# Whole-array gates for one chunk, a shorter first guess, and another choice of tiles in a fused attention and feed-forward kernel

## The chip, the core and the metric

The kernel runs on one core of a Trainium2 chip. The core has a matrix engine (TensorE, PE in the profile; its weight loads are listed as PEld), a vector engine (VectorE, DVE), a scalar engine for functions such as the exponential (ScalarE, ACT), a general engine (GpSimd, POOL) and a queue that issues transfers (SyncE, SP). The engines run at the same time and wait for each other through semaphores. Matmul results go to a memory of eight banks, each 128 partitions by 512 numbers of 32 bits. The metric is the device time of one execution in microseconds (us), the median of several runs.

## What is computed

One transformer block without learned norm weights: attention on normalised `x`, then a gated feed-forward layer on the normalised sum. `S` is 2048, `D` 640, with 32 heads of 20 and a feed-forward width of 1728; inputs and output are bfloat16.

```python
def _A_ref(x, wqkv, wo):
    ...
    scores = jnp.einsum("bhqd,bhkd->bhqk", q, k) * (Dh ** -0.5)
    p = _softmax(scores, axis=-1)
    o = jnp.einsum("bhqk,bhkd->bhqd", p, v)
    return (lambda x, *d: x.transpose(*d))(o, 0, 2, 1, 3).reshape(B, S, D) @ wo

def _B_ref(x, w_gate, w_up, w_down):
    g = jnp.einsum("bsd,df->bsf", x, w_gate)
    u = jnp.einsum("bsd,df->bsf", x, w_up)
    h = _gelu(g) * u
    return jnp.einsum("bsf,fd->bsd", h, w_down)

x = A_x
h = x + _A_ref(_layernorm(x, axis=-1), A_wqkv, A_wo)
h2 = h + _B_ref(_layernorm(h, axis=-1), B_w_gate, B_w_up, B_w_down)
```

## The kernel before

**Chunks, slots, tiles, units.** The 2048 query rows are cut into seven chunks of 512, 512, 256, 256, 256, 128 and 128 rows (`CHUNKS`, numbered 0 to 6). Heads are handled in eight groups of four. A slot is one chunk with as many groups as make 512 columns: eight slots each for chunks 0 and 1, four each for chunks 2 to 4, two each for chunks 5 and 6, 32 in all, numbered 0 to 31. A slot has 64 tiles of scores, each 128 keys by 512 columns, which fill one bank. Tiles are worked in units of two or three neighbouring banks. The string `PATS` (line 766) gives each slot one character: under `2` units of three and two tiles alternate, in banks 0 to 2 and 3 to 4; under `3` all units have three tiles, and the second bank set is 3 to 5.

**Who takes the exponential.** A unit's scores are one group of matmuls on quarter rows of the array (`unit`, line 851), then one ACT exponential over all its banks (line 862). In some units of three the third tile goes to DVE instead, which computes the exponential from integer and polynomial operations (`d_exp`, line 788): a pass out of the bank, then seven operations on a pair of tiles, or on a single one at the end of a slot. The string `DS` (line 767) gives each slot a hexadecimal digit: how many of its tiles go to DVE. They are spread over the slot's whole units of three, without the first and the last two (`d_units`, lines 924 to 932). The exponentials are multiplied with the values on quarter columns of the array (line 912) and summed in bank 6.

**Work in the background.** The projections of later groups and, after the last slot of a chunk, that chunk's output projection, norm and feed-forward layer (`post`, line 979) are mixed into the slots that follow, in the banks that attention leaves free (5 and 7; under `3` only 7). In `post`, `ln_rsqrt` (line 576) gives the inverse square root of the variance: for the input's norm and for the last chunk by ACT and a reciprocal, for chunks 0 to 5 by DVE operations on a few numbers, a first guess from the bits of the number and two rounds of Newton's method. `mms` (line 1036) makes the gate and up projections. Each of their matmuls is given in two forms: `quarters`, four matmuls of 32 output rows each (line 662), and `whole`, one matmul on the whole array (line 659). The planner takes the quarters (`mode="col"`) as long as score matmuls are left, and the whole form (`alt`) after them. The gates go from their bank to memory by a DVE copy (line 1081), and ACT's gelu follows for several banks at once.

**Chunk 5** is the one in `GT` (line 356). Its attention takes slots 28 and 29; its gates run during slots 30 and 31, and its gelu, up and down projections are held back (`later`, line 1124) until after the last exponential, at the head of the tail. The tail also holds all of chunk 6's `post`.

**What sets the order.** A planner at build time (`Sched.schedule`, line 98) walks through time with a fixed cost for each operation, takes the ready operation of the highest priority on each engine (scores and exponentials first, then sums with the values, then epilogues, then background), gives out banks and so fixes the order of each engine's instructions. A change of the array's mode between `row`, `col` and `full` is charged 0.1 us (`MODE_SWITCH`, line 31). On the chip each engine works through its list in that order and waits where something is not ready. [...]

Of the kernel before, what the change touches and what calls it, by code (L numbers as in the profile page):

```python
# [6 lines left out]
ALU = mybir.AluOpType  # L7
# [3 lines left out]
I32 = mybir.dt.int32  # L11
# [39 lines left out]
class Sched:  # L51
# [10 lines left out]
    def op(self, eng, fns, dur, prio, reads=(), writes=(), acq=(), rel=(), after=(), sem=None, lat=None, mode=None, mb=0.0, alt=None):  # L62
        if self.evp is not None and eng == "dve" and rel and prio >= P_EPI:
            prio = self.evp
        o = Op()
        o.i = len(self.ops)
        o.eng, o.dur, o.lat, o.sem = eng, dur, LAT[eng] if lat is None else lat, sem
        o.mode = mode
        o.mb = mb
        o.alt = alt  # L70
        o.tag = writes[0] if writes else None
        o.fns = fns if isinstance(fns, list) else [fns]
        o.prio = (prio, o.i)
        deps = set(after)
        for r in reads:
            if r in self.lw:
                deps.add(self.lw[r])
        for w in writes:
            if w in self.lw:
                deps.add(self.lw[w])  # L80
            deps.update(self.rd.get(w, ()))
        for r in reads:
            self.rd.setdefault(r, []).append(o.i)
        for w in writes:
            self.lw[w] = o.i
            self.rd[w] = []
        deps.discard(o.i)
        o.deps = deps
        o.acq = list(acq)
        o.rel = list(rel)  # L90
        o.succ = []
        o.ready = 0.0
        o.start = None
        o.group = None
        self.ops.append(o)
        return o.i
# [230 lines left out]
RSQRT_MAGIC = float(0x5F3759DF)  # L327
# [25 lines left out]
XLAG = 0.85  # L353
XLG0 = 0.5
HG = 1
GT = (5,)
XPL = 1
KPR = 3.0
# [6 lines left out]
def bass_sequential_preLN__mha_block__glu_gated_geglu__prompt_kernel(  # L365
# [12 lines left out]
    with ExitStack() as es:  # L378
        sc = Sched(nc)
        op = sc.op  # L380
# [4 lines left out]
        def I(method, *args, **kwargs):  # L385
            return lambda eng: getattr(eng, method)(*args, **kwargs)  # L386


        def c_mm(n, passes=1):
            return 0.003 + passes * n / 2400.0  # L390
# [92 lines left out]
        def bank(b, n=512):  # L483
            return PS[:, 512 * b.b:512 * b.b + n]
# [91 lines left out]
        def ln_rsqrt(t0, n, prio, need_nm=0):  # L576
            ts = range(t0, t0 + n)
            y, v = rs[:, t0:t0 + n], mv[:, t0:t0 + n, 1]
            a, b = nw[:, 0, 0:n], nw[:, 1, 0:n]
            vk, rk = [("mv", t) for t in ts], [("rs", t) for t in ts]  # L580
            d = lambda fn, r, w: op("dve", fn, 0.14, prio, reads=r, writes=w)
            if need_nm:

                op("act", I("activation", a, v, ACT.Sqrt, bias=epsc[:, 0:1]), 0.19, prio, mode="sqrt", reads=vk + ["eps"], writes=["nw0", "sd"])
                d(I("reciprocal", y, a), ["nw0"], rk)
                if need_nm == 1:
                    d(I("scalar_tensor_tensor", out=nm[:, t0:t0 + n], in0=y, scalar=-1.0, in1=mv[:, t0:t0 + n, 0],
                        op0=ALU.mult, op1=ALU.mult), rk + vk, [("nm", t) for t in ts])
                return
            d(I("tensor_scalar", a, v, LN_EPS, None, ALU.add), vk, ["nw0"])  # L590
            d(I("tensor_scalar", b.bitcast(I32), a.bitcast(I32), 1, None, ALU.logical_shift_right), ["nw0"], ["nw1"])
            d(I("tensor_scalar", y.bitcast(I32), b.bitcast(I32), -1.0, RSQRT_MAGIC, ALU.mult, ALU.add), ["nw1"], rk)
            for _ in range(2):
                d(I("tensor_tensor", b, y, y, ALU.mult), rk, ["nw1"])
                d(I("scalar_tensor_tensor", out=b, in0=b, scalar=-0.5, in1=a, op0=ALU.mult, op1=ALU.mult),
                  ["nw0", "nw1"], ["nw1"])
                d(I("scalar_tensor_tensor", out=y, in0=b, scalar=1.5, in1=y, op0=ALU.add, op1=ALU.mult),
                  ["nw1"] + rk, rk)

        def ln_apply(eng, src, dst, dkey, t, rkeys, prio):  # L600
# [32 lines left out]
        def sc_id():  # L633
            _id[0] += 1
            return _id[0]
# [4 lines left out]
        for t0 in range(0, NT, 4):  # L640
            sa = [t for t in range(t0, t0 + 4) if LNS[t] == "act"]
            for t in range(t0, t0 + 4):
                (ln_stats_act if t in sa else ln_stats)(x_sb[:, t, :], t, [xkey(t)], P_EPI)
            if sa:
                assert sa == list(range(sa[0], sa[-1] + 1))
                op("dve", I("tensor_scalar", mv[:, sa[0]:sa[-1] + 1, 1], mv[:, sa[0]:sa[-1] + 1, 1], 1.0 / D, None, ALU.mult), 0.14,
                   P_QK, reads=[("mv1", t) for t in sa], writes=[("mv", t) for t in sa])
            ln_rsqrt(t0, 4, P_QK, 1)
            for t in range(t0, t0 + 4):
                e_ops.append(ln_apply(LNE[t], x_sb[:, t, :], xn_p[:, t % 4, :], ("xnp", t % 4), t, [xkey(t)], P_QK))  # L650
                transposes(xn_p[:, t % 4, :], [("xnp", t % 4)], xnT[:, :, t * 128:(t + 1) * 128], ("xnT", t),
                           ALLB, P_EPI, LNV[t])
                e_ops.append(len(sc.ops) - 2)
# [5 lines left out]
        def whole(out, l, r, start, stop):  # L659
            return [lambda eng: eng.matmul(out()[0:l.shape[-1]], l, r, start=start, stop=stop, skip_group_check=True)]  # L660

        def quarters(out, l, r, start, stop):
            m = l.shape[-1]
            return [lambda eng, j=j: eng.matmul(out()[j:j + 32], l[:, j:j + 32], r, start=start, stop=stop,  # L664
                                                tile_position=(0, j), skip_group_check=True) for j in range(0, m, 32)]
# [97 lines left out]
            tiles += [(s_, g, kb, j) for g in gs for kb in range(NT // nk) for j in range(4)]  # L763
            slot_end.append(len(tiles))

        PATS = '22222222222322232222222332223322'
        DS = '06418768558877797888786986867867'
        PAT = [((0, 1, 2), (3, 4, 5)) if PATS[i] == '3' else ((0, 1, 2), (3, 4)) for i in range(len(slots))]
        units, ubank, upos = [], [], []
        i = 0  # L770
# [154 lines left out]
        for s_, (c, gs) in enumerate(slots):  # L925
            us = [u for u, tl in enumerate(units) if len(tl) == 3 and all(x[0] == s_ for x in tl)]
            n = int(DS[s_], 16)
            us = us[1:len(us) - DTAIL]
# [50 lines left out]
        def post(c, banks, tail):  # L979
            p = P_EPI if tail else P_BG - PRE * (c >= PREC)  # L980
            q0, nq = CHUNKS[c]
# [10 lines left out]
            for tt in range(nt):  # L992
# [10 lines left out]
                for hf in range(2):  # L1003
                    bk = Bank(*banks)
# [11 lines left out]
            if tail:  # L1016
                op("act", I("activation", nm[:, 0:1], off0[:], ACT.Gelu_apprx_tanh), 0.06, -1, mode="gelu", reads=["off0"],
                   writes=["pre"], after=(sc.lw["sd"],))
# [5 lines left out]
            p, pre = P_BG - TFIRST * tail, p  # L1024
# [11 lines left out]
            def mms(k, w, wkey, after, p=p):  # L1036
                bk, key = Bank(*banks), ("bk", sc_id())
                for fi in range(min(fn_, NF - k * fn_)):
                    f = k * fn_ + fi
                    mf = min(128, DFF - 128 * f)  # L1040
                    for a in range(NA):
                        st = fi == 0 and a == 0
                        op("pe", quarters(lambda fi=fi: bank(bk)[:, fi * nq:(fi + 1) * nq], w[:, a, f * 128:f * 128 + mf],
                                          hnT[:, a, hb * 128:hb * 128 + nq], a == 0, a == NA - 1),
                           c_mm(nq), p, mode="col", alt=whole(lambda fi=fi: bank(bk)[:, fi * nq:(fi + 1) * nq],
                                                              w[:, a, f * 128:f * 128 + mf], hnT[:, a, hb * 128:hb * 128 + nq],
                                                              a == 0, a == NA - 1), reads=hk + [wkey], writes=[key], acq=[bk] if st else [],
                           after=after if st else ())
                return bk, key

            def wid(k):
                return min(512, NF * nq - 512 * k)
# [16 lines left out]
            else:  # L1069

                cp, gl = [], []
                for k in range(nb):
# [3 lines left out]
                    w_ = wid(k)  # L1076
                    if k >= nb - HG and c not in GT:
                        hold.append((k, bg, kg, m, fv, fk, w_))
# [3 lines left out]
                                 reads=[kg], writes=fk, rel=[bg], after=first))  # L1082
# [39 lines left out]

            if c in GT:
                def later(ba):
                    banks[:] = ba
                    gate_after[:] = [last_exp[0]]
                    rest()
                    down(GDP)
# [8 lines left out]
        if XPL:  # L1137
            op("act", I("activation", nm[:, 0:1], off0[:], ACT.Exp, scale=0.0), 0.06, P_QK, mode="exp", reads=["off0", ("xnT", 15), ("xnT", 14)],
               writes=["xpl", ("nm", 0)])
# [20 lines left out]
        for s_, (c, gs) in enumerate(slots):  # L1160
            if c == 0:
                g = s_
# [70 lines left out]
```

## Time and profile before

| | us |
|---|---|
| runs before, median of 3 | 939.43 |
| lowest, highest | 938.72, 939.8 |
| the profiled execution | 939.73 |
| its span, first to last instruction | 937.9 |

The granted clock of TensorE is 1.0 over the whole span. The parts of the page and the further views of the trace are quoted in the prediction, each where it is used. In them, a group row reads: line, engine, operation, what is written from what, shape, count, then busy time and mean duration in ns, then the engine's idle time before those instructions and what ended it. A timeline row reads: start, length, engine, line, operation, shape, count, and in brackets the idle time before it with its releaser. A row merges neighbours of one kind and shows the first one's shape. `L386` is a helper through which many operations are recorded; there the written and read names tell what it is: `pts<-ps` and `rege<-ps` on ACT are the exponentials, `qt_all,kt_all` on PE are scores, `v_all` sums with the values. `L664` is the quarter form and `L660` the whole form.

### The profile page before, as it was taken

The numbers are of one execution on the slowest core, as the hardware profiler recorded it, in microseconds if no ns is written. First come the engines' busy times: TensorE is split into PE (matmuls) and PEld (weight loads), VectorE is DVE, ScalarE is ACT, GpSimd is POOL, SyncE is SP. The second block draws the span as 40 slices with busy tenths as digits, with TensorE's granted clock in tenths as the row PEclk, the third lists the DMA queues.
The fourth block names the chain that finished last, engine by engine and source line by source line (L and its number), as shares of the span: only waits on it lengthen the run. The fifth ranks groups of instructions, "written<-read, shape, count | busy, mean of one in ns | idle before, by whom it ended". The sixth has DMA issues, their size and how long they took to land.

```text
span 937.9 us, 33402 instructions
## 1 busy us (share of the span) xinstructions
PE 877.7 (94%) x15201; PEld 386.6 (41%) x15203; DVE 794.5 (85%) x1749; ACT 904.2 (96%) x884; POOL 11.2 (1%) x45
## 2 busy tenths in 40 slices
PE   5999999999999989999999999999889999989998
PEld 3433332222233222323343333344445654556666
DVE  8659768999999999688999996988998787898673
ACT  7999999999999999999999999999999999999891
POOL 4000000000000000000000000000000000000000
PEclk9999999999999999999999999999999999999999
DMA  7010000000000160000100000011000010000000
GB/s 253 2 30 2 2 1 2 1 1 2 1 2 2 33 253 2 1 1 17 43 3 1 2 2 2 2 31 26 7 3 3 3 31 17 17 4 3 5 18 15
DMA packets 11820, 19.90 MB, mean 21 GB/s; under 512 B 608, under 2 KB 9760, under 8 KB 11680
## 3 DMA queue, kind: packets, MB, share of 16 engines
q1 hardware_dynamic: 11680, 17.78, 5.7%
q8 instruction: 119, 1.95, 0.9%
q14 instruction: 21, 0.17, 0.1%
HBM read 15.16 MB, written 2.62 MB: 19 GB/s over the span
## 4 chain that ended last, share of the span: by engine, by line
ACT 74%; PE 20%; DVE 4%; POOL 1%; issue 1%; POOLq 0%
ACT pts L386 44%; ACT rege L386 29%; PE ps L664 7%; PE ps L386 7%; PE ps L660 4%; DVE rege L386 2%; PE ps L618 1%; POOL regw L386 1%; DVE stats L386 0%; DVE qt_all L386 0%; PE ps L952 0%; DVE rege L1100 0%; DVE kt_all L694 0%; ACT L1087 0%; ACT rege L1087 0%
## 5 line engine op out<-in xcount | busy, mean ns | idle before, releaser
L386 ACT ACTIVATE pts<-ps 128x1024 bf16<-128x1024 f32 (+1 forms) x482 | 549.3, 1345 | 3.2 <-PE ps L386 3.0
L386 ACT ACTIVATE rege<-ps 128x1024 bf16<-128x1024 f32 (+1 forms) x312 | 363.6, 1328 | 1.4 <-PE ps L386 1.3
L386 PE MATMUL ps<-qt_all,kt_all 32*128 32x256 bf16 (+2 forms) x3584 | 311.2, 288 | 36.1 <-ACT pts L386 16.4
L386 PEld LDWEIGHTS ps<-qt_all,kt_all 32*128 32x128 bf16 x3584 | 96.5, 92 | 275.8 <-ACT pts L386 130.6
L664 PE MATMUL ps<-rege,regw 128*32 128x256 bf16 (+2 forms) x2970 | 158.7, 308 | 5.1 <-issue 2.3
L386 PE MATMUL ps<-pts,v_all 128*21 128x256 bf16 (+2 forms) x1956 | 157.7, 292 | 0.4 <-DVE osb L386 0.3
L386 PE MATMUL ps<-rege,v_all 128*21 128x256 bf16 (+2 forms) x1394 | 129.4, 294 | 0.0
L664 PE MATMUL ps<-regw 128*32 128x512 bf16 (+1 forms) x1656 | 120.5, 358 | 1.0 <-DVE v_all L749 0.5
L386 DVE TENSOR_TENSOR rege<-rege 128x1024 bf16<-128x1024 bf16 (+3 forms) x170 | 108.4, 641 | 1.0
L386 DVE TENSOR_SCALAR qt_all<-ps 128x512 int16<-128x512 f32 x110 | 75.3, 685 | 16.0 <-PE ps L386 15.5
L664 PEld LDWEIGHTS ps<-rege,regw 128*32 128x32 bf16 x2970 | 73.3, 96 | 37.6 <-issue 17.5
L386 DVE TENSOR_SCALAR rege<-rege 128x1024 bf16<-128x1024 int16 (+3 forms) x225 | 87.3, 398 | 1.3
L386 DVE TENSOR_TENSOR qt_all<-qt_all 128x1024 bf16<-128x1024 bf16 (+3 forms) x124 | 82.3, 664 | 1.2
L664 PE MATMUL ps<-regw,rege 128*32 128x320 bf16 x1484 | 79.3, 301 | 0.3 <-DVE rege L1100 0.3
L386 DVE TENSOR_SCALAR rege<-ps 128x512 int16<-128x512 f32 x103 | 70.5, 684 | 9.0 <-PE ps L386 8.5
L386 DVE TENSOR_SCALAR qt_all<-qt_all 128x1024 bf16<-128x1024 int16 (+3 forms) x182 | 73.3, 408 | 1.9
L386 PEld LDWEIGHTS ps<-pts,v_all 128*21 128x21 bf16 x1956 | 46.4, 90 | 60.6 <-issue 52.5
L386 PEld LDWEIGHTS ps<-rege,v_all 128*21 128x21 bf16 x1394 | 38.4, 90 | 42.1 <-issue 35.1
L386 PE MATMUL ps<-wo,gk 128*21 128x256 bf16 x296 | 52.6, 274 | 0.0
L664 PEld LDWEIGHTS ps<-regw 128*32 128x32 bf16 x1656 | 37.8, 95 | 34.8 <-issue 15.9
L1100 DVE TENSOR_TENSOR rege<-rege,ps 128x512 bf16<-128x512 bf16 (+2 forms) x53 | 35.8, 676 | 13.1 <-PE ps L664 12.8
L664 PEld LDWEIGHTS ps<-regw,rege 128*32 128x32 bf16 x1484 | 35.8, 95 | 22.2 <-issue 13.7
(109 smaller groups left out, 727.3 us busy)
## 6 DMA issues: line engine op xcount, KB each, us to landing
rege<-in_A_x_dram SPq DMA_DIRECT2D x11, 320.0 KB, 4.7
out_dram<-rege SPq DMA_DIRECT2D x16, 160.0 KB, 1.9
regw<-in_B_w_gate_dram SPq DMA_DIRECT2D x1, 2160.0 KB, 9.2
regw<-in_B_w_up_dram SPq DMA_DIRECT2D x1, 2160.0 KB, 14.1
regw<-in_B_w_down_dram SPq DMA_DIRECT2D x1, 2080.0 KB, 19.2
rege<-in_A_wqkv_dram SPq DMA_DIRECT2D x1, 1600.0 KB, 9.0
rege<-in_A_x_dram SPq DMA_DIRECT2D x2, 640.0 KB, 4.4
regw<-in_A_wqkv_dram SPq DMA_DIRECT2D x1, 800.0 KB, 8.0
```

Of the source, the lines that this page charges most:

```text
L386: return lambda eng: getattr(eng, method)(*args, **kwargs)
L618: op("pe", lambda eng, a=a: eng.transpose(bank16(bk, D)[:, 128 * a:128 * a + 128], src[:, a * 128:(a + 1) * 128], ident[:]), 0.056, prio, ...
L660: return [lambda eng: eng.matmul(out()[0:l.shape[-1]], l, r, start=start, stop=stop, skip_group_check=True)]
L664: return [lambda eng, j=j: eng.matmul(out()[j:j + 32], l[:, j:j + 32], r, start=start, stop=stop, tile_position=(0, j), skip_group_check=T ...
L1100: hdone.append(op("dve", lambda eng, bu=bu, fv=fv, m=m, w_=w_: eng.tensor_tensor(fv, fv, bank(bu, w_)[0:m, :], ALU.mult), c_dve(w_), p, re ...
```

## The change

Three edits are made. The matmuls of chunk 5's gate and up projections are built in the whole form with mode `full` at once, without the quarter form. In `ln_rsqrt`, the shift of the bits by one and the subtraction from the magic number become one operation, a product with -0.5 and a sum. The strings `PATS` and `DS` are set anew; in 17 slots (1, 2, 10, 12 to 16, 20, 22 to 24, 26 to 29 and 31) the pattern, the number of tiles for DVE or the way the units fall differs. A switch `LNG`, which would put the Newton rounds on GpSimd, is added and is 0, so that branch isn't built.

```diff
+LNG = 0
+LNGT = 0.2
+FW = 1
 GT = (5,)
...
             d(I("tensor_scalar", a, v, LN_EPS, None, ALU.add), vk, ["nw0"])
-            d(I("tensor_scalar", b.bitcast(I32), a.bitcast(I32), 1, None, ALU.logical_shift_right), ["nw0"], ["nw1"])
-            d(I("tensor_scalar", y.bitcast(I32), b.bitcast(I32), -1.0, RSQRT_MAGIC, ALU.mult, ALU.add), ["nw1"], rk)
+            d(I("tensor_scalar", y.bitcast(I32), a.bitcast(I32), -0.5, RSQRT_MAGIC, ALU.mult, ALU.add), ["nw0"], rk)
+            if LNG:
+                g = lambda fn, r, w: op("pool", fn, LNGT, prio, reads=r, writes=w)
+            else:
+                g = d
             for _ in range(2):
-                d(I("tensor_tensor", b, y, y, ALU.mult), rk, ["nw1"])
-                d(I("scalar_tensor_tensor", out=b, in0=b, scalar=-0.5, in1=a, op0=ALU.mult, op1=ALU.mult),
+                g(I("tensor_tensor", b, y, y, ALU.mult), rk, ["nw1"])
...
+                g(I("scalar_tensor_tensor", out=b, in0=b, scalar=-0.5, in1=a, op0=ALU.mult, op1=ALU.mult),
                   ["nw0", "nw1"], ["nw1"])
...
-        PATS = '22222222222322232222222332223322'
-        DS = '06418768558877797888786986867867'
+        PATS = '22222222222332232222223332223222'
+        DS = '03518768559878787888887976887868'
...
-                        op("pe", quarters(lambda fi=fi: bank(bk)[:, fi * nq:(fi + 1) * nq], w[:, a, f * 128:f * 128 + mf],
+                        wh = FW and c in GT
+                        op("pe", (whole if wh else quarters)(lambda fi=fi: bank(bk)[:, fi * nq:(fi + 1) * nq], w[:, a, f * 128:f * 128 + mf],
                                           hnT[:, a, hb * 128:hb * 128 + nq], a == 0, a == NA - 1),
-                           c_mm(nq), p, mode="col", alt=whole(lambda fi=fi: bank(bk)[:, fi * nq:(fi + 1) * nq],
+                           c_mm(nq), p, mode="full" if wh else "col", alt=None if wh else whole(lambda fi=fi: bank(bk)[:, fi * nq:(fi + 1) * nq],
```

More of the change, by code (lines that the diff above doesn't have):

```diff
@@ L590, in ln_rsqrt @@
             d(I("tensor_scalar", a, v, LN_EPS, None, ALU.add), vk, ["nw0"])
-            d(I("tensor_scalar", b.bitcast(I32), a.bitcast(I32), 1, None, ALU.logical_shift_right), ["nw0"], ["nw1"])
-            d(I("tensor_scalar", y.bitcast(I32), b.bitcast(I32), -1.0, RSQRT_MAGIC, ALU.mult, ALU.add), ["nw1"], rk)
-            for _ in range(2):
-                d(I("tensor_tensor", b, y, y, ALU.mult), rk, ["nw1"])
-                d(I("scalar_tensor_tensor", out=b, in0=b, scalar=-0.5, in1=a, op0=ALU.mult, op1=ALU.mult),
+            d(I("tensor_scalar", y.bitcast(I32), a.bitcast(I32), -0.5, RSQRT_MAGIC, ALU.mult, ALU.add), ["nw0"], rk)
[3 more added lines that the diff above has]
+                g = d
+            for _ in range(2):
+                g(I("tensor_tensor", b, y, y, ALU.mult), rk, ["nw1"])
+                if LNG:
+                    g(I("tensor_tensor", b, b, a, ALU.mult), ["nw0", "nw1"], ["nw1"])
+                    g(I("tensor_scalar", b, b, -0.5, 1.5, ALU.mult, ALU.add), ["nw1"], ["nw1"])
+                    g(I("tensor_tensor", y, y, b, ALU.mult), ["nw1"] + rk, rk)
+                    continue
+                g(I("scalar_tensor_tensor", out=b, in0=b, scalar=-0.5, in1=a, op0=ALU.mult, op1=ALU.mult),
                   ["nw0", "nw1"], ["nw1"])
-                d(I("scalar_tensor_tensor", out=y, in0=b, scalar=1.5, in1=y, op0=ALU.add, op1=ALU.mult),
+                g(I("scalar_tensor_tensor", out=y, in0=b, scalar=1.5, in1=y, op0=ALU.add, op1=ALU.mult),
                   ["nw1"] + rk, rk)
```

## The prediction

> **What bounds the kernel now.** I read the page first: its busy times, the chain of waits, the queues.
>
> ```profile
> span 937.9 us, 33402 instructions
> PE 877.7 (94%) x15201; PEld 386.6 (41%) x15203; DVE 794.5 (85%) x1749; ACT 904.2 (96%) x884; POOL 11.2 (1%) x45
> q8 instruction: 119, 1.95, 0.9%
> ACT 74%; PE 20%; DVE 4%; POOL 1%; issue 1%; POOLq 0%
> ```
>
> ScalarE (ACT) is busy for 96% of the span and carries 74% of the chain, so I count in ACT time: its work, and the places where it stands still. Next came busy time by stretches, cut where a slot begins (its first exponential, found by counting the 794 exponentials in order).
>
> ```profile
> core 0: us, PE busy (x) PEld busy (x) DVE busy (x) ACT busy (x) POOL busy (x), PEclk, DMA share, GB/s
> 61.90:89.80 27.90, 25.93 (x372) 9.00 (x371) 24.57 (x54) 26.35 (x26) 0.00 (x0) 1.00 0.08 25
> 302.20:328.20 26.00, 24.57 (x256) 7.39 (x248) 25.29 (x52) 26.00 (x28) 0.00 (x0) 1.00 0.10 28
> 328.20:352.90 24.70, 21.55 (x246) 6.59 (x249) 23.93 (x48) 24.70 (x22) 0.00 (x0) 1.00 0.63 242
> 352.90:379.40 26.50, 25.59 (x305) 7.04 (x299) 23.40 (x48) 26.50 (x28) 0.00 (x0) 1.00 0.00 1
> 847.20:880.40 33.20, 32.20 (x1076) 22.40 (x1071) 27.14 (x58) 33.02 (x32) 0.00 (x0) 1.00 0.02 4
> 880.40:908.40 28.00, 25.66 (x857) 16.45 (x846) 21.71 (x46) 25.50 (x27) 0.00 (x0) 1.00 0.04 10
> ```
>
> These are slots 1, 10, 11, 12, 30 and 31. ACT is full except in slot 1 (1.55 us idle) and slot 31 (2.50 us idle). ACT's timeline shows three holes there:
>
> ```profile
> 89.83 2.37 ACT L386 ACTIVATE pts<-ps 128x1024 bf16<-128x1024 f32 x2 [1.58 <-PE ps L386]
> ...
> 882.65 1.45 ACT L386 ACTIVATE pts<-ps 128x1536 bf16<-128x1536 f32 x1 [1.22 <-PE ps L386]
> ...
> 886.29 1.94 ACT L386 ACTIVATE rege<-ps 128x1024 bf16<-128x1024 f32 x2 [1.27 <-PE ps L386]
> ```
>
> All three wait for TensorE (PE). What held PE in the last two, by the chain of waits and by counts over two stretches:
>
> ```profile
> 880.17 0.89 PE ps L664 x55
> 881.06 0.87 issue
> ...
> 884.55 1.13 issue
> ...
> 878.15:881.50 3.35, 2.85 (x128) 2.03 (x128) 1.28 (x2) 3.17 (x3) 0.00 (x0) 1.00 0.03 5
> 881.50:885.30 3.80, 2.62 (x128) 2.02 (x128) 1.38 (x2) 2.36 (x2) 0.00 (x0) 1.00 0.02 4
> ```
>
> PE stands in "issue", that is, it waits for nothing that the profile shows, in the middle of the quartered gates (L664). Each stretch from one stop to the next holds exactly 128 matmuls and 128 weight loads, 256 instructions. Queue q8 brings instructions: (15201 + 15203) / 119 packets = 255.5 PE instructions in a packet. So PE stops whenever a packet is used up and the next has not come; from the end of the first stop (881.06 + 0.87 = 881.93) to the end of the second (884.55 + 1.13 = 885.68) one packet lasted 3.75 us, a supply of 68 instructions per us.
>
> **The change, part by part.** (a) *Tile choice.* Counting units by the two strings, as the code does: before, 547 exponentials of two tiles and 247 of three (794, 1835 tiles on ACT, 213 on VectorE); after, 538 and 252 (790, 1832 and 216). Prices:
>
> ```profile
> L386 ACT ACTIVATE pts<-ps 128x1024 bf16<-128x1024 f32 x322 | 347.3, 1202 | 1.6 <-PE ps L386 1.6
> L386 ACT ACTIVATE pts<-ps 128x1536 bf16<-128x1536 f32 x160 | 257.3, 1634 | 1.5 <-PE ps L386 1.4
> ...
> 190.86 2.20 ACT L386 ACTIVATE rege<-ps 128x1024 bf16<-128x1024 f32 x2
> 192.72 1.68 ACT L386 ACTIVATE pts<-ps 128x1536 bf16<-128x1536 f32 x1
> ```
>
> Two two-tile exponentials that follow each other start 1.86 us before the next, 0.93 each; a third tile adds 1.634 - 1.202 = 0.43, so 1.36. The change is -9 x 0.93 + 5 x 1.36 = **-1.6 us** of ACT, all of it on the path.
>
> VectorE (DVE) gets three tiles more in sum: slots 2, 10, 13, 20, 22 and 31 gain one, slot 27 two, slot 1 loses three, slots 15 and 24 one each. A pair of tiles is two passes out of PSUM, three tensor-tensor and four tensor-scalar operations:
>
> ```profile
> L386 DVE TENSOR_SCALAR rege<-ps 128x512 int16<-128x512 f32 x50 | 34.1, 682 | 0.7 <-PE ps L386 0.5
> L386 DVE TENSOR_TENSOR rege<-rege 128x1024 bf16<-128x1024 bf16 x46 | 31.2, 683 | 0.2
> L386 DVE TENSOR_SCALAR rege<-rege 128x1024 bf16<-128x1024 int16 x46 | 19.0, 417 | 0.2
> ```
>
> 2 x 0.68 + 3 x 0.68 + 4 x 0.42 = 5.1, about 2.5 us a tile. Slot 1 is relieved of 7.5 us. Its hole has this behind it:
>
> ```profile
> 87.76 0.48 DVE L749 CAST v_all<-ps 128x320 bf16<-128x320 f32 x1
> ...
> 88.30 0.59 PE L664 MATMUL ps<-regw 128*32 128x320 bf16 x12 [0.49 <-DVE v_all L749]
> ```
>
> PE sat on a value projection whose bank DVE had not emptied, and the scores that ACT needed were queued behind it. With 7.5 of 24.57 us gone from DVE there, I take 1.2 of the 1.58 us as gained (between 0 and 1.58; some other operation can be late in the new order): **-1.2**. On the other side, slot 10 has 0.7 us free on DVE and gets 2.5: 1.8 us spill into slots 11 (0.8 free) and 12 (3.1 free). What spills is chunk 0's feed-forward work, which has until slot 13; the passes that free ACT's banks go first. I take +0.3 for all the gaining slots together (0 to +2.2, slot 10's spill with the 0.4 us by which its ACT time shrinks).
>
> At the very end slot 31's eighth DVE tile makes its last one half of a pair; now it is worked alone:
>
> ```profile
> 902.34 0.69 DVE L386 TENSOR_SCALAR qt_all<-ps 128x512 int16<-128x512 f32 x1
> ...
> 907.06 0.29 DVE L386 TENSOR_SCALAR qt_all<-qt_all 128x512 int16<-128x512 int16 x1
> 909.53 0.69 DVE L386 COPY osb<-ps 128x512 f32<-128x512 f32 x1 [0.98 <-PE ps L386]
> ```
>
> Between its pass and its end lie 4.7 us, in which an earlier pair is finished too. As half of a pair it needs 3.7 us after the pass (3 x 0.68 + 4 x 0.42), so the last sum is not later: 0.
>
> (b) *Gates of chunk 5.* 270 quarter matmuls become 70 of the whole array, 540 PE instructions become 140: 400 fewer, at 68 per us 5.9 us of supply, in a place where supply fell short by the 1.22 + 1.27 = 2.5 us that ACT waited. The up projections of that chunk run after the last scores and were whole already. What whole ones cost PE:
>
> ```profile
> L664 PE MATMUL ps<-rege,regw 128*32 128x128 bf16 x270 | 6.7, 220 | 2.3 <-issue 2.3
> ...
> 873.18 0.40 PE L386 MATMUL ps<-rege,v_all 128*21 128x128 bf16 x16
> 873.52 0.34 PE L618 MATMUL ps<-ident,xn_t 128*128 128x128 bf16 x3
> ...
> 876.43 0.40 PE L386 MATMUL ps<-pts,v_all 128*21 128x128 bf16 x16
> 876.67 0.39 PE L664 MATMUL ps<-rege,regw 128*32 128x128 bf16 x16
> ...
> 880.10 0.96 PE L664 MATMUL ps<-rege,regw 128*32 128x128 bf16 x55
> 922.60 8.33 PE L660 MATMUL ps<-rege,regw 128*128 128x128 bf16 x140
> ```
>
> 55 quarters take 0.96 - 0.22 (the last one's own time) = 0.74 us, 54 ns for four; 140 whole ones 8.11, 58 ns each. As a stream the gates get no shorter: 4.1 against 3.6 us. Going from the attention sums to a whole matmul takes 0.34 us from the first of 16, to a quarter 0.24, so each visit costs 0.10 more; some ten visits, 1.0. Together PE loses 1.5 us and wins the stops. Between a gain of 2.5 and, if the stops stay, a loss of 1.5, I take the gain less 0.4, since slot 31 leaves PE 2.3 us to spare: **-2.1**.
>
> [...]
>
> (c) *First guess of the square root.* One small DVE operation goes from each of six calls:
>
> ```profile
> L386 DVE TENSOR_SCALAR nw<-nw x6: 154/160/170, 279.0 to 868.6; 128x2 int32<-128x2 int32 x3, 128x4 int32<-128x4 int32 x2, 128x1 int32<-128x1 int32 x1
> ```
>
> Six times 0.16 is 1.0 us of DVE, ahead of gates that ACT does not wait for: 0 (at most -0.2, the one of chunk 5, close to the gates).
>
> **Sum:** -1.6 - 1.2 + 0.3 - 2.1 = -4.6 us. The profiled execution took 939.7 (span 937.9 and 1.8 around it), 0.3 above the median 939.4 of the runs shown. From that median: 934.8 us.
>
> **Rivals.** *The stops stay or move.* The planner knows nothing of instruction packets; slot 30 runs 1076 + 1071 instructions in 33.2 us, 65 per us, close to the 68. If quartered work of chunk 4 slides into the place of the gates, ACT waits there: -4.6 + 2.1 = -2.5, 936.9. For it: that rate. Against it: slot 30 itself loses ACT only 0.2 us. *DVE is the bound in slots 10 to 12*, and its spill lands on ACT: -4.6 - 0.3 + 2.2 = -2.7, 936.7. Against it: slots 10 and 11 run DVE at 97% now without an idle moment on ACT. [...] *Slower: DVE falls behind its place in the order.* Each engine's order is fixed ahead, so a pass that frees a bank late stops PE's queue and with it ACT, as in slot 1, for 1.58 us. Eight tiles are added in seven slots; if each of the seven loses that, the time is -4.6 - 0.3 + 7 x 1.58 = +6.2, 945.6; it is slower from the fourth such slot on. Against it: slot 31 has 6.3 us free on DVE for the 2.5 that it gains, and slots 10 and 11 show that even a DVE at 97% need not stop ACT. *The change does not do what it says* is possible only in (b), where it is the first rival.
>
> **How the numbers follow.** Forecast 0.63; stops stay 0.17; slots 10 to 12 0.09; drains 0.05; slower 0.06. Bounds: all gains in full -1.6 - 1.58 - 2.5 - 0.2 = -5.9, 933.5; all costs -1.6 + 1.5 + 2.2 = +2.1, 941.5. Below the bound lies one thing more, chunk 4's last matmuls, which stand before the tail's first transposes now and may be done earlier:
>
> ```profile
> 909.42 1.12 PE L660 MATMUL ps<-regw,rege 128*128 128x320 bf16 x7
> ```
>
> Of that 1.1 us I allow 0.7. The range 932.8 to 938.0 holds the forecast and the first three rivals. A measurement of this kernel tells about 0.2%, 1.9 us, from no change. The two rivals at -2.5 and -2.7 lie near that line and give a third of their 0.26 to no change: faster 0.85, same 0.09, slower 0.06.
>
> **What would show it.** Right: 790 exponentials; no hole of ACT over 0.3 us between 870 and 908; no hole in slot 1; the gates as some 70 matmuls of L660 ahead of the last exponential, with no "issue" piece near 1 us among them; the last exponential about 4.6 us earlier and the tail behind it as long as now, 29.5 us. Wrong: ACT waiting for PE in slots 10 to 13 or 27 to 31, or stops every 256 PE instructions in another place.

## The result and the profile after

The changed kernel takes 935.29 us (median of 5 runs, 934.89 to 935.88) against 939.43 (938.72 to 939.8): a ratio of 0.9955, 95% interval 0.9944 to 0.9966, or 4.1 us less. The forecast was 934.8. The profiled execution's span is 933.6, 4.3 us shorter.

The page of the changed kernel, with the lines that answer to those of before (`L389` is the helper that was `L386`, `L671` the whole form that was `L660`, `L675` the quarter form that was `L664`):

```profile
span 933.6 us, 32923 instructions
PE 875.7 (94%) x14957; PEld 385.6 (41%) x14959; DVE 797.7 (85%) x1760; ACT 902.1 (97%) x880; POOL 11.1 (1%) x45
ACT 85%; PE 10%; DVE 3%; POOL 1%; issue 0%; POOLq 0%
L389 ACT ACTIVATE pts<-ps 128x1024 bf16<-128x1024 f32 (+1 forms) x485 | 553.3, 1361 | 0.3
L389 ACT ACTIVATE rege<-ps 128x1024 bf16<-128x1024 f32 (+1 forms) x305 | 363.4, 1363 | 0.4 <-PE ps L389 0.4
```

The same two groups on the page of before:

```profile
L386 ACT ACTIVATE pts<-ps 128x1024 bf16<-128x1024 f32 (+1 forms) x482 | 549.3, 1345 | 3.2 <-PE ps L386 3.0
L386 ACT ACTIVATE rege<-ps 128x1024 bf16<-128x1024 f32 (+1 forms) x312 | 363.6, 1328 | 1.4 <-PE ps L386 1.3
```

794 exponentials became 790. ACT's idle time ahead of them, the last number but the releaser, fell from 3.2 + 1.4 = 4.6 us to 0.7, and ACT's share of the chain rose from 74 to 85%. ACT's busy time fell from 904.2 to 902.1.

The timeline of ACT shows where the attention phase ends: the table load that follows the last exponential. Before:

```profile
32.86 3.71 ACT L386 ACTIVATE pts<-ps 128x1536 bf16<-128x1536 f32 x3
...
908.39 1.28 ACT L386 ACT_TABLE_LOAD   x1
```

After:

```profile
33.10 3.71 ACT L389 ACTIVATE pts<-ps 128x1536 bf16<-128x1536 f32 x3
...
79.42 4.71 ACT L389 ACTIVATE pts<-ps 128x1536 bf16<-128x1536 f32 x4
...
902.69 1.28 ACT L389 ACT_TABLE_LOAD   x1
```

The phase from first to last exponential is 875.5 us before and 869.6 after, 5.9 us less: 2.1 of ACT work and 3.9 of holes. The tail behind it is 937.9 - 908.4 = 29.5 us before and 933.6 - 902.7 = 30.9 after, 1.4 us more. The first exponential starts 0.2 later. -5.9 + 1.4 + 0.2 = -4.3. So a quarter of what ACT won was given back in the tail. What the tail has more of stands in PE's timelines: chunk 4's down projections (whole matmuls of 320 columns), which fill PE while it waits for the epilogue. Before there are 21 of them (the seven at 909.42 stand in the prediction):

```profile
906.72 1.23 PE L660 MATMUL ps<-regw,rege 128*128 128x320 bf16 x7
...
908.22 0.72 PE L660 MATMUL ps<-regw,rege 128*128 128x320 bf16 x4
...
910.82 0.67 PE L660 MATMUL ps<-regw,rege 128*128 128x320 bf16 x3
```

After there are 34, and then the tail's PE work runs through almost without a gap:

```profile
900.96 1.33 PE L671 MATMUL ps<-regw,rege 128*128 128x320 bf16 x7
...
902.55 0.85 PE L671 MATMUL ps<-regw,rege 128*128 128x320 bf16 x5
...
903.90 1.12 PE L671 MATMUL ps<-regw,rege 128*128 128x320 bf16 x7
...
905.39 1.77 PE L671 MATMUL ps<-regw,rege 64*128 64x320 bf16 x11
...
907.16 0.81 PE L671 MATMUL ps<-regw,rege 128*128 128x320 bf16 x4
...
914.08 4.29 PE L671 MATMUL ps<-regw,rege 128*128 128x320 bf16 x28 [0.22 <-DVE rege L1112]
```

Thirteen more, at (4.29 - 0.30) / 28 = 0.14 us each (the last one's own 0.30 taken off), are 1.9 us of PE. 1.4 of them show; the rest went into gaps of PE in this stretch (0.37 and 0.52 us before, 0.22 after).

Busy time by stretches after, for slots 1, 10, 11, 12, 30 and 31:

```profile
62.20:89.90 27.70, 27.20 (x409) 9.73 (x401) 19.70 (x46) 27.57 (x27) 0.00 (x0) 1.00 0.08 25
301.90:327.40 25.50, 23.89 (x256) 7.03 (x248) 24.67 (x53) 25.50 (x27) 0.00 (x0) 1.00 0.11 33
327.40:352.10 24.70, 21.60 (x233) 7.44 (x235) 24.46 (x52) 24.70 (x22) 0.00 (x0) 1.00 0.62 237
352.10:378.70 26.60, 24.10 (x295) 7.84 (x287) 23.10 (x46) 26.60 (x23) 0.00 (x0) 1.00 0.01 2
844.80:877.90 33.10, 31.83 (x976) 21.97 (x969) 26.78 (x57) 33.04 (x33) 0.00 (x0) 1.00 0.01 3
877.90:902.70 24.80, 24.37 (x685) 15.51 (x683) 22.18 (x46) 24.78 (x27) 0.00 (x0) 1.00 0.02 4
```

ACT (the fourth busy time) is full in all of them. Slot 31 shrank from 28.0 to 24.8 us; PE is now busy for 24.37 of those, against 25.66 of 28.0.

### The profile page after: what moved, and what is told of

Same layout as the page of the kernel before. It is cut to its first block, busy times and chain, and to the rows that moved or that the text cites. A ratio compares the mean times of both kernels' runs of the same rounds, so it can differ in the third digit from the quotient of the medians.

```text
span 933.6 us, 32923 instructions
## 1 busy us (share of the span) xinstructions
PE 875.7 (94%) x14957; PEld 385.6 (41%) x14959; DVE 797.7 (85%) x1760; ACT 902.1 (97%) x880; POOL 11.1 (1%) x45
## 4 chain that ended last, share of the span: by engine, by line
ACT 85%; PE 10%; DVE 3%; POOL 1%; issue 0%; POOLq 0%
ACT pts L389 51%; ACT rege L389 33%; PE ps L671 4%; PE ps L675 3%; PE ps L389 3%; DVE qt_all L389 1%; PE ps L629 1%; DVE rege L389 1%; POOL regw L389 1%; ACT L389 0%; ACT L1099 0%; DVE stats L389 0%; DVE rege L1093 0%; ACT rege L1099 0%; DVE rege L1112 0%
## 5 line engine op out<-in xcount | busy, mean ns | idle before, releaser
L389 ACT ACTIVATE pts<-ps 128x1024 bf16<-128x1024 f32 (+1 forms) x485 | 553.3, 1361 | 0.3
L389 ACT ACTIVATE rege<-ps 128x1024 bf16<-128x1024 f32 (+1 forms) x305 | 363.4, 1363 | 0.4 <-PE ps L389 0.4
L389 PE MATMUL ps<-qt_all,kt_all 32*128 32x256 bf16 (+2 forms) x3584 | 309.5, 288 | 36.0 <-ACT pts L389 15.5
L389 PEld LDWEIGHTS ps<-qt_all,kt_all 32*128 32x128 bf16 x3584 | 96.8, 92 | 271.0 <-ACT pts L389 125.5
L675 PE MATMUL ps<-rege,regw 128*32 128x256 bf16 (+1 forms) x2700 | 155.1, 317 | 3.4 <-DVE qt_all L744 0.8
L389 PE MATMUL ps<-pts,v_all 128*21 128x256 bf16 (+2 forms) x1948 | 157.6, 293 | 0.2 <-DVE osb L389 0.2
L389 PE MATMUL ps<-rege,v_all 128*21 128x256 bf16 (+2 forms) x1396 | 127.5, 294 | 0.0
L675 PE MATMUL ps<-regw 128*32 128x512 bf16 (+1 forms) x1656 | 120.7, 359 | 0.2 <-DVE kt_all L705 0.2
L389 DVE TENSOR_TENSOR rege<-rege 128x1024 bf16<-128x1024 bf16 (+2 forms) x172 | 111.7, 652 | 0.9
L389 DVE TENSOR_SCALAR rege<-rege 128x1024 bf16<-128x1024 int16 (+3 forms) x227 | 89.1, 404 | 1.4
L389 DVE TENSOR_SCALAR qt_all<-ps 128x512 int16<-128x512 f32 x112 | 76.9, 686 | 11.8 <-PE ps L389 11.4
L389 DVE TENSOR_TENSOR qt_all<-qt_all 128x1024 bf16<-128x1024 bf16 (+3 forms) x127 | 82.5, 650 | 1.2
L675 PEld LDWEIGHTS ps<-rege,regw 128*32 128x32 bf16 x2700 | 67.7, 96 | 37.6 <-issue 13.7
L389 DVE TENSOR_SCALAR qt_all<-qt_all 128x1024 int16<-128x1024 int16 (+3 forms) x187 | 74.0, 402 | 1.4
L389 DVE TENSOR_SCALAR rege<-ps 128x512 int16<-128x512 f32 x104 | 71.2, 685 | 2.0 <-PE ps L389 1.4
L389 PEld LDWEIGHTS ps<-pts,v_all 128*21 128x21 bf16 x1948 | 46.3, 90 | 60.4 <-issue 51.4
L675 PE MATMUL ps<-regw,rege 128*32 128x320 bf16 (+1 forms) x1432 | 70.8, 301 | 0.4 <-DVE rege L1129 0.3
L389 PEld LDWEIGHTS ps<-rege,v_all 128*21 128x21 bf16 x1396 | 37.8, 90 | 41.9 <-issue 35.6
L389 PE MATMUL ps<-wo,gk 128*21 128x256 bf16 x291 | 51.4, 274 | 0.0
L675 PEld LDWEIGHTS ps<-regw 128*32 128x32 bf16 x1656 | 37.2, 95 | 34.1 <-issue 16.4
L675 PEld LDWEIGHTS ps<-regw,rege 128*32 128x32 bf16 (+1 forms) x1432 | 34.7, 96 | 20.3 <-issue 10.1
```

## The experiments

Two theories of the gates stood against each other. *Supply*: PE used up its packets of 256 instructions faster than the next came (one in 3.75 us), and fewer instructions cure it. *Form*: the stops come from the order or the banks, and each step from the attention sums to a whole matmul costs PE 0.10 us more than one to a quarter (0.34 against 0.24 us); the expectations call this cost the drains. The first three kernels keep every engine's order of work as it was and change only the form in which chunk 5's gates are emitted (in the second, its up projections as well).

**The old order with whole gates** (the kernel before otherwise):

```diff
-                        op("pe", quarters(lambda fi=fi: bank(bk)[:, fi * nq:(fi + 1) * nq], w[:, a, f * 128:f * 128 + mf],
+                        op("pe", (whole if c in GT else quarters)(lambda fi=fi: bank(bk)[:, fi * nq:(fi + 1) * nq], w[:, a, f * 128:f * 128 + mf],
```

> The kernel before with every engine's order as it was; only the form of chunk 5's gate matmuls differs: 70 whole ones are emitted where 270 quarters stood. Theory (instruction supply): 400 PE instructions fewer are 5.9 us of supply at 68 per us, so the two holes of ACT before 882.65 and 886.29 (1.22 + 1.27 us) go, and the time falls by 2.0 to 2.5 us, to about 937.2. Rival (the quarters are no cause, the drains count): the holes stay or grow, and the time is 939.4 to 940.9.

937.71 us against 939.72 for the kernel before on that chip, ratio 0.998 (0.9971 to 0.9989): 2.0 us less. Of the two holes this is left in ACT's timeline:

```profile
883.98 1.94 ACT L386 ACTIVATE rege<-ps 128x1024 bf16<-128x1024 f32 x2 [0.23 <-PE ps L386]
```

The 1.22 and 1.27 us became 0.23 in one place, with no other change in the order. In PE's timeline the step to a whole matmul takes what the prediction counted for it:

```profile
876.68 0.40 PE L386 MATMUL ps<-pts,v_all 128*21 128x128 bf16 x16
877.02 0.40 PE L660 MATMUL ps<-rege,regw 128*128 128x128 bf16 x4
```

0.34 us from the first attention sum to the first whole gate, 0.10 more than to a quarter. The 0.23 us that ACT still waits fall in a stretch in which PE is busy without a break (3.80 of 3.80 us from 881.50 to 885.30), so they can come from these steps; the trace does not separate them from PE's other work.

**The new order with quarters** (the changed kernel otherwise):

```diff
-                        op("pe", (whole if wh else quarters)(lambda fi=fi: bank(bk)[:, fi * nq:(fi + 1) * nq], w[:, a, f * 128:f * 128 + mf],
+                        op("pe", quarters(lambda fi=fi: bank(bk)[:, fi * nq:(fi + 1) * nq], w[:, a, f * 128:f * 128 + mf],
```

> The changed kernel with every engine's order as it was; only chunk 5's gates are emitted as 270 quarters in the place of 70 whole matmuls. Theory (instruction supply): PE stops every 256 instructions among the gates again, ACT gets holes of 2.0 to 2.5 us in all, and the time rises from 935.3 to 937.3 to 937.8. Rival (order and drains): without the drains the time stays at 935.3 or falls, down to 934.3.

938.43 us against 939.72 for the kernel before beside it, ratio 0.9985 (0.9976 to 0.9994). The changed kernel's 935.29, with its ratio of 0.9955, was taken in another set of runs: the difference is 3.1 us as the times stand and 2.8 by the ratios. The theory's 937.3 to 937.8 was passed by 0.6. ACT's timeline has two holes again:

```profile
879.39 1.45 ACT L389 ACTIVATE rege<-ps 128x1536 bf16<-128x1536 f32 x1 [0.91 <-PE ps L389]
...
887.08 1.02 ACT L389 ACTIVATE rege<-ps 128x1024 bf16<-128x1024 f32 x1 [0.61 <-PE ps L389]
```

They are 1.5 us together, less than the 2.0 to 2.5 expected. The other half is in the tail, which the expectation left out: the edit also makes quarters of chunk 5's up projections, which run after the last exponential. PE's timeline there:

```profile
911.24 2.53 PE L675 MATMUL ps<-rege,regw 128*32 128x128 bf16 x168
915.13 1.35 PE L675 MATMUL ps<-rege,regw 128*32 128x128 bf16 x74 [1.36 <-issue]
```

A run of quarters with nothing between them stops once for 1.36 us. 1.5 + 1.36 = 2.9 us, as much as the difference.

**The old order with eighths** (the kernel before, each quarter cut into two matmuls of 64 columns):

```diff
+eighths = lambda out, l, r, start, stop: [lambda eng, j=j, x=x: eng.matmul(out()[j:j + 32, x:x + r.shape[-1] // 2], l[:, j:j + 32], r[:, x:x + r.shape[-1] // 2], start=start, stop=stop, tile_position=(0, j), skip_group_check=True) for x in (0, r.shape[-1] // 2) for j in range(0, l.shape[-1], 32)]
...
-                        op("pe", quarters(lambda fi=fi: bank(bk)[:, fi * nq:(fi + 1) * nq], w[:, a, f * 128:f * 128 + mf],
+                        op("pe", (eighths if c in GT else quarters)(lambda fi=fi: bank(bk)[:, fi * nq:(fi + 1) * nq], w[:, a, f * 128:f * 128 + mf],
```

> The kernel before with every engine's order as it was; each quarter matmul of chunk 5's gates is cut into two of 64 columns, so that 540 matmuls with their weight loads (1080 instructions) stream the same columns as 270 did. Theory (instruction supply): 540 instructions more are 7.9 us of supply at 68 per us; PE stops at some five packets and not three, ACT's holes in slots 30 and 31 grow from 2.5 to between 6 and 10 us, and the time is 943 to 947. Rival (the columns streamed, or the bank that the next gate waits for, set the pace): the same columns and the same banks, so at most 1 us more, 939.4 to 940.4.

946.4 us against 939.72, ratio 1.0071 (1.0058 to 1.0084): 6.7 us more for the same columns. ACT's waits between 860 and 920 in this kernel:

```profile
ACT pts L386 <- PE ps L386: 5.1, 4, 2.8
ACT rege L386 <- PE ps L386: 2.8, 4, 1.8
```

7.9 us where the holes were 2.5. The chain of waits of the same kernel (`L631` is the new form):

```profile
878.73 0.23 PE ps L631 x5
...
881.30 0.89 issue
882.20 0.48 PE ps L631 x37
...
883.93 1.73 issue
885.67 0.65 PE ps L631 x45
...
888.91 0.23 issue
889.14 0.98 PE ps L631 x53
```

The stops end at 878.73, 882.20, 885.67 and 889.14, always 3.47 us apart. Busy time by stretches, cut inside the stops:

```profile
882.00:885.50 3.50, 1.74 (x128) 1.47 (x128) 0.00 (x0) 1.16 (x2) 0.00 (x0) 1.00 0.02 5
885.50:889.10 3.60, 3.24 (x128) 2.51 (x128) 1.38 (x2) 2.04 (x2) 0.00 (x0) 0.56 0.02 5
```

From one stop to the next are again 128 matmuls and 128 weight loads, whether they keep PE busy for 1.74 us or for 3.24: in these stretches PE runs at the pace of its instruction packets. One thing more differs from the kernel before. The granted clock (the number behind the five busy times) was 0.56 in the second of these stretches and 0.84 from 889.20 to 900.00. So a part of the 6.7 us can be a slower PE instead of missing instructions; how much was not separated. The supply theory holds in all three kernels, with the number of instructions taken away (0.23 us of ACT's holes left among the gates), put back (1.5) and doubled (7.9).

The next four take the edits apart; each is planned anew.

**The strings alone** (in the kernel before):

```diff
-        PATS = '22222222222322232222222332223322'
-        DS = '06418768558877797888786986867867'
+        PATS = '22222222222332232222223332223222'
+        DS = '03518768559878787888887976887868'
```

> The kernel before with the two new strings alone; gates in quarters and the old first guess, and an order planned anew. Theory (the terms of the sum): 1.6 us less work on ACT and the hole of 1.58 us in slot 1 gone, while some 2.5 us of holes among chunk 5's gates stay: -2.5 to -3.2, 936.2 to 936.9. Rival (slots 10 to 13 or the new order on DVE give it back): ACT has holes there of 2 us or more, and the time is 938 or more.

947.41 us against 939.72, ratio 1.0084 (1.0071 to 1.0098): 7.7 us *more*. The theory fell, and so did the rival, since ACT has no hole over 0.6 us in its attention phase, and that phase even ends early. ACT's timeline:

```profile
882.64 1.28 ACT L1087 ACT_TABLE_LOAD   x1
...
903.57 1.28 ACT L386 ACT_TABLE_LOAD   x1
```

The attention phase ends 4.8 us earlier than before, but the tail is 945.6 (this run's span) - 903.6 = 42.0 us. Chunk 4's gelu starts at 882.64; in the kernel before the same load stands at 862.45. PE's timeline shows the work that came too late:

```profile
908.67 1.69 PE L660 MATMUL ps<-rege,regw 128*128 128x256 bf16 x14
...
911.55 3.09 PE L660 MATMUL ps<-rege,regw 128*128 128x256 bf16 x36
...
916.25 7.01 PE L660 MATMUL ps<-regw,rege 128*128 128x320 bf16 x45
```

Chunk 4's up projections (256 columns) and its down projections are still to be done after the last exponential.

**All but the first guess** (the changed kernel with the old two operations):

```diff
-            d(I("tensor_scalar", y.bitcast(I32), a.bitcast(I32), -0.5, RSQRT_MAGIC, ALU.mult, ALU.add), ["nw0"], rk)
+            d(I("tensor_scalar", b.bitcast(I32), a.bitcast(I32), 1, None, ALU.logical_shift_right), ["nw0"], ["nw1"])
+            d(I("tensor_scalar", y.bitcast(I32), b.bitcast(I32), -1.0, RSQRT_MAGIC, ALU.mult, ALU.add), ["nw1"], rk)
```

> The changed kernel (new strings, whole gates) with the old first guess of two operations. Theory (the sum by parts): six small DVE operations more cost 0 to 0.2 us, 935.3 to 935.5. Rival (the strings hold for one plan only): the planner's order falls out otherwise, chunk 4's gelu comes some 20 us later as with the strings alone, its up and down projections land in the tail, and the time is 944 to 948.

947.28 us against 940.12 for the kernel before beside it, 7.2 more, and 12.0 more than the changed kernel's 935.29 from another set of runs, for six operations of 0.16 us. The rival holds: the gelu of chunk 4 starts as late as with the strings alone.

```profile
882.82 1.28 ACT L1100 ACT_TABLE_LOAD   x1
...
903.34 1.28 ACT L389 ACT_TABLE_LOAD   x1
```

**The first guess alone** (in the kernel before):

```diff
-            d(I("tensor_scalar", b.bitcast(I32), a.bitcast(I32), 1, None, ALU.logical_shift_right), ["nw0"], ["nw1"])
-            d(I("tensor_scalar", y.bitcast(I32), b.bitcast(I32), -1.0, RSQRT_MAGIC, ALU.mult, ALU.add), ["nw1"], rk)
+            d(I("tensor_scalar", y.bitcast(I32), a.bitcast(I32), -0.5, RSQRT_MAGIC, ALU.mult, ALU.add), ["nw0"], rk)
```

> The kernel before with the shorter first guess alone. Theory (the sum by parts): 0 to -0.2 us, 939.2 to 939.5. Rival (the strings hold for one plan only): six small operations fewer give another order throughout, and the time moves by 1 us or more, to 940.5 or later.

940.21 us against 940.12, ratio 1.0002 (0.9992 to 1.0011): no change that can be told. The size of the term was right.

**The gates alone** (whole and planned in mode `full`, in the kernel before):

```diff
-                        op("pe", quarters(lambda fi=fi: bank(bk)[:, fi * nq:(fi + 1) * nq], w[:, a, f * 128:f * 128 + mf],
+                        op("pe", (whole if c in GT else quarters)(lambda fi=fi: bank(bk)[:, fi * nq:(fi + 1) * nq], w[:, a, f * 128:f * 128 + mf],
...
-                           c_mm(nq), p, mode="col", alt=whole(lambda fi=fi: bank(bk)[:, fi * nq:(fi + 1) * nq],
+                           c_mm(nq), p, mode="full" if c in GT else "col", alt=None if c in GT else whole(lambda fi=fi: bank(bk)[:, fi * nq:(fi + 1) * nq],
```

> The kernel before with chunk 5's gates whole, planned in mode full; old strings, old first guess. Theory (instruction supply): as with the whole form in the old order, the holes among the gates go and the time falls by 1.7 to 2.5 us, to 937.0 to 937.8. Rival (a new order undoes it): more of chunk 4's work is left after the last exponential and the tail grows by 1 us or more, 938.5 or later.

937.05 us against 940.12, ratio 0.9967 (0.9955 to 0.9979): 3.1 us less, more than expected. ACT has no hole left in slots 30 and 31; the timeline ends in the table load at

```profile
905.21 1.28 ACT L386 ACT_TABLE_LOAD   x1
```

which is 3.2 us earlier than before, and the tail is 934.9 - 905.2 = 29.7 us. Slot 31 takes 25.2 us here (879.98 to 905.20), nearly as short as in the changed kernel, and PE is busy for 25.00 of them; yet only 24 whole down projections of chunk 4 are counted as above, three more than before.

**Slot 1 with three DVE tiles** (the kernel before, the digit of `DS` for slot 1 being 3 and not 6):

```diff
-        DS = '06418768558877797888786986867867'
+        DS = '03418768558877797888786986867867'
```

> The kernel before with three instead of six DVE tiles in slot 1 alone. Theory (DVE holds up PE's queue in slot 1): the hole of ACT of 1.58 us near 88 is gone or under 0.3 us, ACT works 3 tiles = 1.3 us longer, in sum -0.3 us (939.1). Rival (the hole has another cause, a wait in PE's order): it stays, and the time is 1.3 us longer, 940.7.

939.35 us against 940.12, ratio 0.999 (0.9981 to 1.0): in time not clearly apart from no change, as the theory's -0.3 would have it. The profile decides. ACT's busy time on the page rose from 904.2 to 905.5 us, the 1.3 of three tiles. Where the hole of 1.58 us was, ACT's timeline now has rows without an idle time in brackets:

```profile
86.04 3.75 ACT L386 ACTIVATE pts<-ps 128x1536 bf16<-128x1536 f32 x3
89.66 2.38 ACT L386 ACTIVATE rege<-ps 128x1024 bf16<-128x1024 f32 x2
```

A new plan by itself does not remove the hole: with the gates alone and with the first guess alone, both planned anew with the old digit, it is 1.59 us.

The last two ask whether there is more to be had.

**Strings once more** (the changed kernel with strings for which the plan leaves less of PE's work to the tail):

```diff
-        PATS = '22222222222332232222223332223222'
-        DS = '03518768559878787888887976887868'
+        PATS = '22222222222332222222222322222222'
+        DS = '12518768559878888788898988886868'
```

> The changed kernel with the two strings chosen once more for it, so that the plan keeps less of PE's work for the time after the last exponential. Counted: 592 exponentials of two tiles, 214 of three and one of one, 1827 tiles, by the prices of the sum 1.0 us less ACT work than in the changed kernel. Theory (time = ACT's work up to the last exponential + PE's work left behind it): ACT's part 1.0 us shorter and the tail about 1 us shorter, 933.0 to 933.8 against 935.3. Rival (what the planner doesn't know, instruction packets and late DVE passes, gives it back): new holes of ACT of 2 us or more, 935 or later.

934.0 us (933.05 to 934.21) against 939.77 for the kernel before beside it, ratio 0.9935 (0.9923 to 0.9947); the changed kernel's 0.9955 was taken in another set of runs, and the two intervals just overlap. The runs themselves, 933.05 to 934.21 and 934.89 to 935.88, do not. It is 0.2 us above the expected range, and ACT's part did not get shorter as counted: its end stands at

```profile
902.82 1.28 ACT L389 ACT_TABLE_LOAD   x1
```

against 902.69, with a first exponential 0.4 later, so the phase is 0.3 us shorter where 1.0 was counted. The gain is in the tail, 932.3 - 902.8 = 29.5 us against 30.9: 10 whole down projections of chunk 4 are left for the end, where the changed kernel has 34. It is the fastest kernel of the study.

**The same with chunk 4 whole too** (order kept; up and down matmuls of chunk 4 emitted whole):

```diff
-                            op("pe", quarters(lambda bk=bk: bank(bk, 320), ha_f[0:mf, o:o + 128],
+                            op("pe", (whole if c == 4 else quarters)(lambda bk=bk: bank(bk, 320), ha_f[0:mf, o:o + 128],
...
-                        op("pe", (whole if wh else quarters)(lambda fi=fi: bank(bk)[:, fi * nq:(fi + 1) * nq], w[:, a, f * 128:f * 128 + mf],
+                        op("pe", (whole if wh or c == 4 and wkey == "wu" else quarters)(lambda fi=fi: bank(bk)[:, fi * nq:(fi + 1) * nq], w[:, a, f * 128:f * 128 + mf],
```

> The same with every engine's order kept, but chunk 4's up and down matmuls emitted whole too. Theory (instruction supply binds wherever quartered background meets attention in slots 28 to 31): if the kernel with the new strings still has holes of ACT or stops of PE there, they go, and the time falls by their sum, up to 1 us. Rival (only chunk 5's gates were short of instructions; the drains count): 0.10 us more for each visit, 0 to 1 us slower than that kernel.

935.16 us, 1.2 more than with quarters there (934.0, both beside the same runs of the kernel before). The rival holds. With quarters there PE was already busy for 27.77 of the last 27.82 us of the phase (from 875.00 on), so the supply does not bind there, and there were no stops to win. What the whole form costs stands in PE's timelines. A visit after attention sums, with quarters:

```profile
899.55 0.40 PE L389 MATMUL ps<-pts,v_all 128*21 128x128 bf16 x16
899.78 0.44 PE L675 MATMUL ps<-regw,rege 128*32 128x320 bf16 x8
```

The same visit with whole matmuls:

```profile
900.62 0.40 PE L389 MATMUL ps<-pts,v_all 128*21 128x128 bf16 x16
900.95 0.44 PE L671 MATMUL ps<-regw,rege 128*128 128x320 bf16 x2
```

The whole matmuls start 0.33 us after the first of the sums, the quarters 0.23, and both then take 0.44. About ten visits after 874 differ so, by some 0.10 each, which is 1.0 of the 1.2 us; the last exponential ends 1.15 us later, and the tail is no longer.

## Why the prediction was right, and what in it was not

**The gates, -2.1: right in mechanism, a little small.** 2.5 us of holes went in the changed kernel, and the time fell by 2.0 us in the old order and by 3.1 with the gates planned alone. The instruction supply was argued from two counts of 256; taking instructions away, putting them back and doubling them showed it. Of the 0.4 us kept back for PE's losses nothing shows in the changed kernel, where ACT has no hole among the gates; in the old order the 0.23 us that was left of the holes may be theirs. The forecast also gives drains a chance of 0.05. No run shows PE draining; what the runs show is 0.10 us more for a step from the attention sums to a whole matmul, and a gain of 2.0 us in the old order, where the 2.5 us of holes less all of the 1.5 us counted as PE's loss would have been 1.0.

**The tile choice, -1.6 of ACT work:** ACT's busy time fell by 2.1.

**Slot 1, -1.2:** the hole went from 1.58 to 0.13, so 1.45; that DVE's load was the cause was tried by its own edit. The relief itself was over-counted: DVE is busy for 19.70 us in the slot and was for 24.57, 4.9 less and not 7.5.

**Slots 10 to 12, +0.3:** nothing. ACT is busy for all of 25.50, 24.70 and 26.60 us, though DVE is at 97 and 99% in the first two. Nothing of a spill held ACT up there.

**Slot 31's last DVE tile, 0:** the 4.7 us are counted from start to start. From the end of its pass (902.34 + 0.69) to the end of its last operation (907.06 + 0.29) it is 4.3, still more than the 3.7 it was compared with.

**The first guess, 0:** right by itself. What the prediction did not see is that the parts do not add up. Alone, they measure -3.1 (gates), +7.7 (strings) and +0.1 (guess), +4.7 in sum; together -4.1. The forecast counted what the changed kernel's own strings do within their own plan, and that count held because all three edits came together. It was no statement about the strings alone, and the expectation that made one of it failed by 10 us.

**The tail, "as long as now": wrong.** This is the step that failed: the tail grew by 1.4 us, and the prediction had even allowed 0.7 for a shorter one. It had no term for background that is left over when the phase gets shorter. Thirteen more of chunk 4's down projections ran behind the last exponential, where PE sets the end. The shorter slot 31 does not explain that by itself: with the gates alone it took 25.2 us, against 24.8 here, and only three more were left, with a tail of 29.7. And with the strings chosen once more, the phase ends at 902.8 as here, and the tail is 29.5. So it goes with the plan that these strings give; what in that plan puts the matmuls so late was not followed. That the errors nearly cancel (holes and ACT work 5.9 us less where 4.6 were forecast, 1.4 back in the tail) is luck, and it is why 934.8 lies so close to 935.3.

Of the rivals, *the stops stay or move* was excluded by the profile (no wait of PE in the changed kernel, from the first exponential on, is put down to "issue"), the 0.10 us more for each step to a whole matmul cost ACT nothing that shows (it is busy for 33.04 of 33.10 us in slot 30 and 24.78 of 24.80 in slot 31), and all of ACT's holes in the attention phase make 0.7 us, so the slower case did not come near. That strings could go wrong through the tail, with ACT running full, was none of the rivals.

## What to carry to other kernels

Here many small matmuls with their weight loads outran a supply of 68 instructions per us. The sign was idle time of PE put down to "issue" (0.87 and 1.13 us) that recurred every 256 instructions, and larger instructions cured it (2.0 us less in the old order), though one whole matmul took 58 ns and the four quarters in its place 54. Cure only where the stops are: the same edit on chunk 4's longer matmuls cost 1.2 us. Where two engines are both nearly full, count what a new plan leaves for the time behind the last work of one of them, and do not price one edit of a jointly chosen set by itself.

## What the runs showed that was not expected

PE's instruction packets came 3.75 us apart in the kernel before and 3.47 us apart in the one with eighths (68 and 74 instructions per us). What sets that difference was not tried.

A plan can turn on six operations of 0.16 us: with the new strings, leaving the old first guess in moved chunk 4's gelu from 858 to 883 us and cost 12.0 us, while in the old strings' plan the same edit cost nothing. How that delay builds up from chunk to chunk was not followed by experiment.
